# Four constants and the table of settings of a kernel's build-time scheduler: attention and token-mixing MLP on one core

## The chip, the cores and the metric

The kernel runs on one core of a Trainium2 chip. The metric is the device time of one execution in microseconds (us); less is better. TensorE (PE) multiplies matrices, ScalarE (ACT) evaluates activation functions, VectorE (DVE) and GpSimd (POOL) do elementwise work, and SyncE (SP) issues the DMA transfers. Each engine executes its own list of instructions strictly in the order in which the program gives them; between engines there are only semaphores.

## The reference

With x of 2048 rows and 512 columns, 32 heads of 16 columns and F = 1376:

```python
def _A_ref(x, wqkv, wo):
    qkv = (x @ wqkv).reshape(B, S, 3, H, Dh).transpose(2, 0, 3, 1, 4)
    q, k, v = qkv[0], qkv[1], qkv[2]
    p = softmax(einsum("bhqd,bhkd->bhqk", q, k) * Dh ** -0.5)
    o = einsum("bhqk,bhkd->bhqd", p, v)
    return o.transpose(0, 2, 1, 3).reshape(B, S, D) @ wo

def _B_ref(x, w1, b1, w2, b2):
    u = gelu(einsum("bsd,sf->bdf", layernorm(x), w1) + b1)
    return (einsum("bdf,fs->bds", u, w2) + b2).transpose(0, 2, 1)

xn = layernorm(x)
return x + _A_ref(xn, A_wqkv, A_wo) + _B_ref(xn, B_w1, B_b1, B_w2, B_b2)
```

## The kernel before

The work is cut into score steps, numbered 0 to 1023. One step is one tile of 128 keys against 512 queries for two heads: two matmuls of 32 by 128 weights (line 792), each into one bank of PSUM. Two steps make four matmuls that run side by side in the four row strips of TensorE. Thirty-two steps, which are 16 key tiles of four heads, are a block; there are 32 blocks of 512 queries and four heads each. The last block works in two halves of 256 queries (line 782 for its scores).

A finished step then needs its exponentials, 128 x 1024 values, and it can get them in two ways:

- on ScalarE: one activation over both banks when the two banks are neighbours, or two activations of 512 columns each when they are not (line 818). I call such a step an A step.
- on VectorE: one pass that writes the bits of an approximate exponential as 16-bit integers (line 827), followed by three integer "shifts" of that tile (line 833), which give three more terms of the approximation. The shifts may run on VectorE or on GpSimd. I call such a step a D step.

TensorE then multiplies each resulting tile with V (line 874, and line 863 in the last block): four matmuls of 128 by 32 weights over 256 columns, side by side in the four column strips. An A step needs one such group, a D step needs four. Between the scores and this "PV" work lie other column-strip matmuls: projections of Q, K and V and both products of the MLP and the output projection (line 922, in groups of four over 512 columns, and line 978). Changing between the row strips of the scores and the column strips of all else is a mode switch. Lines 715 and 719 are filler matmuls that keep the clock of TensorE up.

The Python program decides the whole order while it is being built. The class `Sched` keeps a clock per engine, a model of what each operation costs, and a main loop that always takes the candidate with the earliest modelled start. The constants of this model stand at the head of the file. `PE_SWITCH` is the cost of a mode switch, `PE_LAT` the time from the start of a matmul of 512 columns to the moment at which its reader may start, the third entry of a `cost=("C", ...)` tuple the time of a matmul group, and `port_time` says when VectorE or GpSimd may start an operation that uses the port that they share. A wrong constant changes no result: the semaphores enforce every dependency. It changes only which operation comes next in the lists.

The choices of the loop have seven knobs. They decide when a step is given to VectorE, how many tile buffers are kept back, how close to ScalarE's next need the scores are put, whether other matmuls come ahead of PV work, how much work VectorE may have waiting, and how many D steps are open at a time. `POLICIES` has 16 sets of the seven. `PLAN` has 64 hexadecimal digits, one for each 16 score steps, and each digit names the set in force during those steps:

```python
d_steal, p_keep, dead_slack, pe_fit, ext_rank, d_back, d_fly = POLICIES[PLAN[plan_at // PLAN_STEP]]
```

The next scores are placed at a time worked out from ScalarE's modelled clock; other matmuls are taken first if they end before it:

```python
need = sc.free["act"] + EXP_I * ahead - 0.46 - dead_slack
go = max(e_s, min(need, t2))
if pick is not None and pick[0] + pick[4] + PE_SWITCH <= go + pe_fit:
    pe_c = pick[:4]
```

Scores of a block may not start before the PV work of the block before the last has been placed in full. When a block's PV work is complete, an epilogue (lines 1096 to 1132) copies it out, divides by the sums, and leaves it for the output projection. The last block has its own end (lines 1141 to 1189).

Of the kernel before, what the change touches and what calls it, by code (L numbers as in the profile page):

```python
# [56 lines left out]


SEM = 0.05
PE_SWITCH = 0.11  # L60
PE_LAT = 0.40
AS_I, AS_L = 0.8, 0.9
EXP_I, EXP_L = 0.904, 1.03
EXPH_I, EXPH_L = 0.477, 0.60
# [25 lines left out]
PLAN_STEP = 16  # L90
PLAN = tuple(int(c, 16) for c in "61cb9804b04216e61600920a2d300db6900a621963f2325ed3a2bc440e00e3d2")
URGENT = ("kv0", "qt", "kt", "vt")
URG_DUE = 24
UT0, UT_STEP = 196, 31
# [29 lines left out]
class Sched:  # L124
# [51 lines left out]
    def keep_clock(self, ready, cost):  # L176
# [3 lines left out]
        if mode != self.pe_mode:  # L180
            t = max(t, self.pe_end + PE_SWITCH)
        for x in tiles:
# [3 lines left out]
        own = "F" if self.pe_mode in ("F", None) else "C"  # L186
        s = self.pe_end + (PE_SWITCH if own != self.pe_mode else 0.0)
        most = int((t - s - (PE_SWITCH if own != mode else 0.0) - FILL_SLACK) / FILL_T)
        have = self.worked(t - HAM_W, t)
# [41 lines left out]

    def port_time(self, eng, t):

        return max(t, self.port_free["pool" if eng == "dve" else "dve"])

    def _time(self, op, cost, ready, port):
        eng = op.eng
# [6 lines left out]
        elif eng == "pe":  # L244
            mode, tiles, dur = cost
            t = max(self.free["pe"], ready)
            if mode != self.pe_mode:
                t = max(t, self.pe_end + PE_SWITCH)
                self.pe_mode = mode
# [7 lines left out]
            self.busy["pe"] += dur * len(tiles) / 4.0  # L257
            op.t0, op.t1 = t, t + dur + PE_LAT - 0.214
            self.pe_work.append((t, dur, len(tiles) / 4.0))
# [122 lines left out]
def bass_parallel_sum__softmax_full_mha__mixer_token_mlp__prompt_kernel(  # L382
# [18 lines left out]
    with ExitStack() as es:  # L401
# [56 lines left out]
        def bank(i):  # L458
            return ps[:, i * 512:(i + 1) * 512]
# [280 lines left out]
        def blk_of(n):  # L740
            if n < 4 * N_TURN:
                kt, b = n // 4, n % 4 // 2
            elif n < 2 * BN:
                b, kt = divmod(n // 2 - 2 * N_TURN, NKT - N_TURN)
                kt += N_TURN
            else:
                b, kt = divmod(n // 2, NKT)
            qb, G = divmod(b, NG)
            T, e_ = divmod(G, 2)
            return b, kt, qb, G, T, e_  # L750
# [3 lines left out]
        def vblk(n):  # L754
            if 4 * N_TURN > n and n % 4 >= 2:
                return -1
            return blk_of(n)[0] if n < N31 else NBLK - 1 + (n - N31) // 16
# [53 lines left out]
        def buf(i, a=0, z=1024):  # L811
            return pT[:, i, a:z] if i < NPB else x_sb[:, :, :].rearrange("p t d -> p (t d)")[:, 1024 * (i - NPB) + a:1024 * (i - NPB) + z]
# [35 lines left out]
        def pv_specs(item, first, last):  # L848
            n, term, p = item
            b, kt, qb, G, T, e_ = blk_of(n)  # L850
            par = n % 2
            vt, vk = (VM, "VM") if term == len(SHIFTS) else (V17, "V")
            spill = (vk, kt, T + 1) if T < 3 else (vk, kt + 1, 0)
            specs = []
            if n >= N31:
                m = (n - N31) % 16
                pb = vblk(n)
                for z in range(2):
                    k_ = 2 * (m // 2) + z
                    for i in range(2):  # L860
                        c = 2 * par + i
                        off = (k_ * H + 8 * T + 2 * c + e_) * 17
                        specs.append(dict(eng="pe", fn=lambda e, c=c, z=z, i=i, off=off: e.matmul(
                            bank(pv_bank[pb])[32 * c:32 * c + 32, 0:256], lhsT=vt[:, off:off + 32],
                            rhs=buf(p, 512 * i + 256 * z, 512 * i + 256 * z + 256), start=first and z == 0, stop=last and z == 1,
                            tile_position=(0, 32 * c)),
                            reads=[(vk, k_, T), ("pT", p), ("pTh", p), ("Vone",), (vk, k_ + 1, 0)], writes=[("bank", pv_bank[pb])], name="pv",
                            cost=("C", (c,), 0.107)))
                return specs
            vb = vblk(n)  # L870
            for c in range(4):
                h, i = divmod(c, 2)
                off = (kt * H + 8 * T + 4 * par + 2 * i + e_) * 17
                specs.append(dict(eng="pe", fn=lambda e, c=c, h=h, i=i, off=off: e.matmul(  # L874
                    bank(pv_bank[vb])[32 * c:32 * c + 32, 256 * par:256 * par + 256], lhsT=vt[:, off:off + 32],
                    rhs=buf(p, 512 * i + 256 * h, 512 * i + 256 * h + 256), start=first, stop=last,
                    tile_position=(0, 32 * c)),
                    reads=[(vk, kt, T), ("pT", p), ("pTh", p), ("Vone",), spill], writes=[("bank", pv_bank[vb])], name="pv",
                    cost=("C", (c,), 0.107)))
            return specs  # L880

        def pv_emit(b, item):
            pv_q[b].remove(item)
            n, term, p = item
            sk = b if b < NBLK - 1 else (b, n % 2)
            first = sk not in pv_started
            pv_started.add(sk)
            pv_left[b] -= 1
            last = pv_left[b] == 0
            if b >= NBLK - 1:  # L890
                par_done[sk] = par_done.get(sk, 0) + 1
                last = par_done[sk] == 8 + 3 * sum(1 for z in on_d if vblk(z) == b and z % 2 == n % 2) and all(
                    z in pbuf or z in on_d for z in range(NN) if z >= N31 and vblk(z) == b and z % 2 == n % 2)
            for s_ in pv_specs(item, first, last):
                add(s_)
            pv_seen.add((b, n % 2))
            if not (term == 0 and shifts_of.get(n, 0) > 0):
                free_p.append(p)
            else:
                w_hold[n] = p  # L900
# [29 lines left out]
        def score_has(n):  # L930
            b, kt, qb, G, T, e_ = blk_of(n)
            return ("q", b - b % 2) in have and (("k", T, kt // 4) in have if T else ("k0", kt) in have)
# [392 lines left out]
        def grp(b):  # L1325
            return max(0, b)
# [39 lines left out]
        def est(specs):  # L1366
            s0 = specs[0]
            r = 0.0
            for s_ in specs:
                r = max(r, sc.ready(s_["eng"], s_["reads"], s_["writes"]))  # L1370
            t = max(sc.free[s0["eng"]], r)
            if s0.get("port"):
                t = sc.port_time(s0["eng"], t)
            return t
# [102 lines left out]
        while True:  # L1477
            if next_n >= plan_at and plan_at < NN:
                d_steal, p_keep, dead_slack, pe_fit, ext_rank, d_back, d_fly = POLICIES[PLAN[plan_at // PLAN_STEP]]
                plan_at += PLAN_STEP  # L1480
# [21 lines left out]
            if ready_q and fly < d_fly and len(free_p) >= 4 + p_keep:  # L1502
                act_free = sc.free["act"]
                for qi, n in enumerate(ready_q):
# [3 lines left out]
                    t = est(sp_)  # L1508
# [41 lines left out]
            t_pe = max(sc.free["pe"], sc.pe_end)  # L1550
            t_c = max(sc.free["pe"], min(sc.pe_tiles.values()) if sc.pe_tiles else 0.0) if sc.pe_mode == "C" else t_pe + PE_SWITCH
            if next_n < NN and pv_grp >= grp(vblk(next_n)) - 1 and len(free_banks) >= 2 + spare and score_has(next_n):
# [4 lines left out]
                if sc.pe_mode != "S":  # L1557
                    e_s = max(e_s, sc.pe_end + PE_SWITCH)
            jobs = []
# [230 lines left out]
```

## Time and profile before

| | |
|---|---|
| median of 3 runs | 701.61 us (701.22 to 702.15) |
| the profiled execution | 701.73 us |
| its span on the core, first to last instruction | 699.9 us |
| TensorE, line 792 (scores) | 272.5 us busy, 1976 matmuls |
| TensorE, line 874 on pT and V (largest group of PV) | 243.9 us busy, 4588 matmuls |
| VectorE, line 827 (D steps) | 261.1 + 106.5 us busy, 342 instructions |
| VectorE, line 833 (shifts) | 124.2 + 56.9 + 51.2 + 13.0 us busy, 583 instructions |
| GpSimd, line 833 (shifts) | 168.0 + 78.2 + 67.8 + 16.7 us busy, 317 instructions |
| granted clock of TensorE | 1.000 |

Busy times are the union of an engine's spans, so for a pipelined engine they are less than count times mean duration: ScalarE's and TensorE's instructions overlap their neighbours, and how fast an engine really goes is read from the distance of successive ends. "Idle before" is the time in which an engine had nothing running just ahead of an instruction, with what ended it.

### The profile page before, as it was taken

What the parts mean: (1) busy time and instruction counts of PE and PEld (TensorE: products, weight loads), DVE (VectorE), ACT (ScalarE), POOL (GpSimd) and SP (SyncE); (2) the same over time, 40 slices, a digit from 0 to 9 for tenths busy, and PEclk for the clock granted to TensorE, in tenths of its full rate; (3) what the DMA queues carried; (4) which work ended last, traced back from release to release, by engine and by line L of the source; (5) the groups of instructions that cost most, each with busy time, mean ns of one, the idle gap of its engine ahead of it and who ended that gap; (6) DMA issues with size and microseconds to landing.
All of it is one profiled execution on the core that took longest, in us unless ns stands there. A gap on an engine that the chain in (4) does not pass through costs nothing.

```text
span 699.9 us, 30143 instructions
## 1 busy us (share of the span) xinstructions
PE 687.6 (98%) x13277; PEld 319.4 (46%) x13277; DVE 658.0 (94%) x1154; ACT 681.0 (97%) x778; POOL 402.9 (58%) x450
## 2 busy tenths in 40 slices
PE   8999999999999999999999999999999999999998
PEld 6554444454444444444444443444443444444444
DVE  6898979989989999999999999899999999999997
ACT  6999999999999999999999999999999999999995
POOL 5856646765535556565555555565565655656553
PEclk9999999999999999999999999999999999999999
DMA  7500131001322212220222112221112122103101
GB/s 219 81 16 18 48 81 24 21 13 25 79 43 52 45 25 48 49 48 22 42 57 65 40 46 64 62 57 38 35 48 46 30 55 61 47 24 75 26 17 43
DMA packets 88997, 33.88 MB, mean 48 GB/s; under 512 B 70754, under 2 KB 88866, under 8 KB 88866
## 3 DMA queue, kind: packets, MB, share of 16 engines
q1 hardware_dynamic: 88050, 31.56, 19.5%
q8 instruction: 104, 1.70, 1.0%
q10 hardware_dynamic: 816, 0.39, 0.2%
q14 instruction: 27, 0.22, 0.1%
HBM read 21.70 MB, written 2.35 MB: 34 GB/s over the span
## 4 chain that ended last, share of the span: by engine, by line
PE 57%; ACT 29%; DVE 10%; POOL 1%; issue 1%; DMA 1%; POOLq 0%
PE ps L792 21%; PE ps L874 20%; ACT pT L818 20%; PE ps L922 13%; ACT x_sb L818 9%; DVE pT L827 3%; DVE pT L833 2%; DVE x_sb L827 2%; PE ps L978 1%; DMA xnT<-hx 1%; DVE x_sb L833 1%; ACT wkv_raw L1034 1%; PE ps L696 0%; PE ps L1262 0%; PE ps L782 0%
## 5 line engine op out<-in xcount | busy, mean ns | idle before, releaser
L818 ACT ACTIVATE pT<-ps 128x1024 bf16<-128x1024 f32 (+1 forms) x550 | 523.1, 1134 | 4.9 <-PE ps L792 4.8
L792 PE MATMUL ps<-QT,KT 32*128 32x512 bf16 x1976 | 272.5, 385 | 4.3 <-DVE pT L827 1.1
L827 DVE TENSOR_SCALAR pT<-ps 128x1024 int16<-128x1024 f32 (+1 forms) x244 | 261.1, 1081 | 11.9 <-PE ps L792 11.3
L874 PE MATMUL ps<-pT,V 128*32 128x256 bf16 x4588 | 243.9, 275 | 1.6 <-DVE V L988 0.4
L833 POOL TENSOR_SCALAR pT<-pT 128x1024 int16<-128x1024 int16 x161 | 168.0, 1043 | 122.7 <-DVE pT L833 75.5
L818 ACT ACTIVATE x_sb<-ps 128x1024 bf16<-128x1024 f32 (+1 forms) x206 | 223.8, 1173 | 0.9 <-PE ps L792 0.8
L792 PEld LDWEIGHTS ps<-QT,KT 32*128 32x128 bf16 x1976 | 76.2, 91 | 177.6 <-ACT pT L818 72.2
L874 PEld LDWEIGHTS ps<-pT,V 128*32 128x32 bf16 x4588 | 110.8, 96 | 74.2 <-issue 54.7
L833 DVE TENSOR_SCALAR pT<-pT 128x1024 int16<-128x1024 int16 x297 | 124.2, 442 | 0.8
L827 DVE TENSOR_SCALAR x_sb<-ps 128x1024 int16<-128x1024 f32 (+1 forms) x98 | 106.5, 1097 | 5.2 <-PE ps L792 4.7
L874 PE MATMUL ps<-x_sb,V 128*32 128x256 bf16 x1708 | 110.8, 275 | 0.4
L833 POOL TENSOR_SCALAR pT<-x_sb 128x1024 int16<-128x1024 int16 x75 | 78.2, 1043 | 50.1 <-DVE pT L833 30.6
L833 POOL TENSOR_SCALAR x_sb<-pT 128x1024 int16<-128x1024 int16 x65 | 67.8, 1043 | 45.6 <-DVE pT L833 31.5
L874 PE MATMUL ps<-pT,VM 128*32 128x256 bf16 x888 | 63.0, 275 | 0.0
L922 PE MATMUL ps<-hx,wblk 128*32 128x512 bf16 x688 | 58.2, 384 | 0.0
L833 DVE TENSOR_SCALAR pT<-x_sb 128x1024 int16<-128x1024 int16 x139 | 56.9, 433 | 0.2
L874 PEld LDWEIGHTS ps<-x_sb,V 128*32 128x32 bf16 x1708 | 44.2, 96 | 24.1 <-issue 17.8
L833 DVE TENSOR_SCALAR x_sb<-pT 128x1024 int16<-128x1024 int16 x116 | 51.2, 449 | 0.5
L922 PE MATMUL ps<-wkv_raw,wblk 128*32 128x512 bf16 x512 | 42.5, 384 | 0.0
L1132 POOL TENSOR_TENSOR oT<-oC,denb 128x256 bf16<-128x256 f32 (+1 forms) x32 | 23.3, 727 | 27.0 <-DVE pT L833 21.7
L874 PEld LDWEIGHTS ps<-pT,VM 128*32 128x32 bf16 x888 | 23.6, 96 | 12.1 <-issue 9.3
L922 PEld LDWEIGHTS ps<-hx,wblk 128*32 128x32 bf16 x688 | 15.6, 95 | 21.2 <-issue 17.4
(124 smaller groups left out, 466.1 us busy)
## 6 DMA issues: line engine op xcount, KB each, us to landing
wblk<-in_B_w_dram SPq DMA_DIRECT2D x10, 512.0 KB, 5.1
wblk<-in_B_w_dram SPq DMA_DIRECT2D x16, 320.0 KB, 3.7
oC<-OT SPq DMA_DIRECT2D x248, 16.0 KB, 1.8
denb<-rden_scratch SPq DMA_DIRECT2D x124, 32.0 KB, 2.4
xr<-in_A_x_dram SPq DMA_DIRECT2D x16, 128.0 KB, 2.3
out_dram<-osb SPq DMA_DIRECT2D x16, 128.0 KB, 1.9
QT<-Qall SPq DMA_DIRECT2D x120, 16.0 KB, 1.8
x_sb<-in_A_x_dram SPq DMA_DIRECT2D x2, 512.0 KB
```

What stands on the lines that cost most here:

```text
L792: specs.append(dict(eng="pe", fn=lambda e, r=r, bk=bk: e.matmul(bank(bk), lhsT=KT[32 * r:32 * r + 32, T, 128 * kt:128 * (kt + 1)], rhs=QT[ ...
L818: return [dict(eng="act", fn=lambda e, cs=cs, src=src: e.activation(buf(pbuf[n])[:, cs], src, ACTF.Exp, scale=LN2_128), reads=[("bank", k) ...
L827: return [dict(eng="dve", fn=lambda e, cs=cs, src=src: e.tensor_scalar(buf_i(w)[:, cs], src, IBIAS, 0.0, ALU.add, ALU.max), reads=[("bank" ...
L833: return dict(eng=eng, fn=lambda e: e.tensor_scalar(buf_i(o), buf_i(w), float(SHIFTS[k]), 1.0, ALU.add, ALU.mult), reads=[("pT", w), ("pTh ...
L874: specs.append(dict(eng="pe", fn=lambda e, c=c, h=h, i=i, off=off: e.matmul(bank(pv_bank[vb])[32 * c:32 * c + 32, 256 * par:256 * par + 25 ...
L922: specs.append(dict(eng="pe", fn=lambda e, c=c, w=w: e.matmul(bank(ex)[32 * c:32 * c + w, :], lhsT=lhs_of(32 * c, 32 * c + w), rhs=rhs, st ...
L978: specs.append(dict(eng="pe", fn=lambda e, ct=ct, c=c, i=i, t=t: e.matmul(bank(ex)[32 * c:32 * c + 32, 128 * i:128 * (i + 1)], lhsT=xnT[:, ...
L1034: yield "act", [dict(eng="act", fn=lambda e, ap=ap: e.activation(ap, ap, ACTF.Gelu_apprx_tanh), reads=[("gT", ft) for ft in fts], writes=[ ...
L1132: yield "pool", [dict(eng="pool", fn=lambda e, cs=cs: e.tensor_tensor(oT[0:m, qb % NOT, T, cs], oC32[0:m, tb_, cs], denb[0:m, tb_, cs], AL ...
```

## The change

The change gives three constants of the model new values, adds one constant, and replaces all the digits of `PLAN`. Nothing else is touched: the sets in `POLICIES`, the operations and the dependencies are the same. Since the lists are worked out from the model, the order of all engines' instructions changes from the first score steps on, and so does the share of the steps that goes to VectorE.

```diff
-PE_SWITCH = 0.11
-PE_LAT = 0.40
+PE_SWITCH = 0.10
+PE_LAT = 0.38
+PV_T = 0.1095
+POOL_AFTER = 0.03
...
-PLAN = tuple(int(c, 16) for c in "61cb9804b04216e61600920a2d300db6900a621963f2325ed3a2bc440e00e3d2")
+PLAN = tuple(int(c, 16) for c in "0005cfbded1bc0b612a3be2c69463c106436663136cad93cd0c524c434c2215b")
...
     def port_time(self, eng, t):
 
-        return max(t, self.port_free["pool" if eng == "dve" else "dve"])
+        return max(t, self.port_free["pool"] if eng == "dve" else self.port_free["dve"] + POOL_AFTER)
...
-                            cost=("C", (c,), 0.107)))
+                            cost=("C", (c,), PV_T)))
...
-                    cost=("C", (c,), 0.107)))
+                    cost=("C", (c,), PV_T)))
```

## The prediction

> **What bounds the kernel now.** I read the shares first, then the groups of ScalarE, then its list in time. The page's shares and groups:
>
> ```profile
> PE 687.6 (98%) x13277; PEld 319.4 (46%) x13277; DVE 658.0 (94%) x1154; ACT 681.0 (97%) x778; POOL 402.9 (58%) x450
> ...
> L818 ACT ACTIVATE pT<-ps 128x1024 bf16<-128x1024 f32 (+1 forms) x550 | 523.1, 1134 | 4.9 <-PE ps L792 4.8
> ...
> L818 ACT ACTIVATE x_sb<-ps 128x1024 bf16<-128x1024 f32 (+1 forms) x206 | 223.8, 1173 | 0.9 <-PE ps L792 0.8
> ```
>
> Three engines look full, and the chain of waits puts 57% on PE. But PE's busy time is a union of modelled, pipelined spans, and the scheduler fits PE's other work in until ScalarE's next need. ScalarE's exponentials have only 5.8 us of idle ahead of them. ScalarE's list in time around one loss (start, length, xcount):
>
> ```profile
> 223.96 7.58 ACT L818 ACTIVATE pT<-ps 128x1024 bf16<-128x1024 f32 x8
> 231.22 1.24 ACT L818 ACTIVATE x_sb<-ps 128x1024 bf16<-128x1024 f32 x1
> 232.12 4.00 ACT L818 ACTIVATE pT<-ps 128x1024 bf16<-128x1024 f32 x4
> 235.73 1.31 ACT L818 ACTIVATE x_sb<-ps 128x1024 bf16<-128x1024 f32 x1
> 236.64 1.32 ACT L818 ACTIVATE pT<-ps 128x1024 bf16<-128x1024 f32 x1
> 237.54 1.33 ACT L818 ACTIVATE x_sb<-ps 128x1024 bf16<-128x1024 f32 x1
> 239.25 6.52 ACT L818 ACTIVATE pT<-ps 128x1024 bf16<-128x1024 f32 x7 [0.38 <-PE ps L792]
> ```
>
> Ends follow each other by 0.917 us (232.46 to 236.12 for four). Over the trace the 1024-column activation has that distance at its median and 75th percentile, 0.918 at the 90th; the 512-column one 0.490. So ScalarE is the bound, and the span can be written as: first exponential of line 818 starts at 14.3; 684 x 0.917 + 72 x 0.490 = 662.5; the four Gelus and the table load before them 6.5 (357.35 to 363.82); lost time 9.1, of which 0.9 is the table load after the Gelus and the first activation behind it; last exponential ends at 692.6, and 7.4 follow. That makes 699.8 of 699.9.
>
> The 8.15 us really lost: where? TensorE and VectorE at the loss above:
>
> ```profile
> 237.04 0.44 PE L792 MATMUL ps<-QT,KT 32*128 32x512 bf16 x4
> ...
> 237.41 1.48 PE L922 MATMUL ps<-hx,wblk 128*32 128x512 bf16 x24
> 237.47 1.23 DVE L827 TENSOR_SCALAR pT<-ps 128x1024 int16<-128x1024 f32 x1
> 237.54 1.33 ACT L818 ACTIVATE x_sb<-ps 128x1024 bf16<-128x1024 f32 x1
> ...
> 238.82 0.49 PE L792 MATMUL ps<-QT,KT 32*128 32x512 bf16 x4
> ```
>
> Two steps are scored, one becomes a D step, so ScalarE has one exponential, 0.917 us, for the 1.78 us until TensorE scores again. I therefore counted, in the order of each engine's instructions, the runs of other matmuls between two scorings, and priced a run by the trace's start distances: 0.1095 for four PV matmuls, 0.2155 for four of line 922, 0.055 for four over 128 columns, and 0.2 for its two mode switches with what hangs on them (last score to first PV matmul 0.315, PV to score 0.205), plus 0.2 for the scores. Outside the Gelus the order has 42 runs over 1.5 us. Fourteen of them follow a pair with a D step, and at those fourteen places, and no others, ScalarE loses over 0.2 us: eight runs of 1.59 lose 0.38 to 0.59 (mean 0.482), four of 1.70 lose 0.499 on the mean, two of 1.81 lose 0.615; 7.08 in all. The 28 that follow two A steps lose at most 0.1. Twelve shorter runs (1.16 to 1.28) behind a D step lose 0.80 together, 0.067 each, the largest 0.165.
>
> **The change, part by part.** The built program gives exact counts; no time of the scheduler's model is used.
>
> (1) ScalarE's load. Activations of 1024 columns go from 684 to 694, of 512 columns from 72 to 56: +10 x 0.917 - 16 x 0.490 = +1.3 us, straight on the bound. Steps given to VectorE fall from 300 to 298.
>
> (2) Long runs behind a D step: from 14 to 5 (three of 1.59, one of 1.70, one of 1.81). By the rows above they lose 3 x 0.482 + 0.499 + 0.615 = 2.6 instead of 7.1: -4.5. Long runs behind two A steps fall from 28 to 21 and cost nothing, the two queued exponentials (1.83 us) cover them; were that cover gone, each would cost about 0.5.
>
> (3) Middle runs (1.16 to 1.49) behind one A step: from 12 to 27. Some follow a single scored step, which the trace of before has only up to 1.07 us. 23 lie within 1.16 to 1.28; I take 0.067 for each, 1.5. Four, of 1.38 to 1.49, have no row: bounds are 0 and the 0.482 of the 1.59 runs, and I take 0.27, halfway between the neighbours, 1.1. Together 2.6 against 0.8: +1.8. Bounds of the difference: 0 if they lose as much in all as the twelve did, +4.9 if each of the 23 loses 0.165 and each of the four 0.482.
>
> (4) The other engines. TensorE: 24 PV matmuls (-0.66) and 18 fillers (-0.3) fewer, but 1,375 instead of 1,358 runs of one mode, 17 switches x 0.1 = +1.7: +0.7 us, hidden behind ScalarE; uncovered it is all on the end. VectorE: 258 to 251 wide and 84 to 94 half passes of line 827 (distances 1.13 and 0.60) and three shifts of 0.335 fewer: -2.9 us. GpSimd: three shifts of 1.04 fewer, with 42% of its span idle. The SP list keeps its 685 entries and no transfer changes size; no wait of line 792 on a transfer shows in the trace. Cost: 0, no gain either, since ScalarE does not wait for them.
>
> (5) The end. Behind the last exponential the chain of before reads (start, length):
>
> ```profile
> 692.19 0.73 POOL oT L1132
> 692.91 0.04 issue
> 692.96 0.77 POOLq L401
> 693.72 0.04 issue
> 693.77 3.23 PE ps L922 x56
> 697.00 0.02 issue
> 697.03 0.69 DVE osb L1141
> ```
>
> GpSimd's last product comes late because VectorE still has the shifts of step 1019, and four output tiles (0.69 each) are all added behind it. In the new order the last D step is 1016, that product is placed before step 1022 is scored, and one output tile is added before the last PV group and one right behind it. Two additions off the chain are worth up to 1.3; bounds 0 and -1.3, I take -0.7.
>
> (6) The start. The first D step is 18 instead of 24, while VectorE still does layer norms: one pass and three shifts, 1.1 + 1.0 us, earlier. ScalarE's first 21 exponentials run without idle now, and VectorE waits 0.72 us at 27.3 within them, so I take 0; bounds 0 and +1.0.
>
> Sum: +1.3 - 4.5 + 1.8 - 0.7 = -2.1 us. Against the profiled execution: 701.7 - 2.1 = 699.6; its time stands 0.1 above the median of the runs, so the median becomes 699.5 us.
>
> The Trainium skill, TensorEngine Tiling (Array Packing), Key Properties, speaks against the change: changing the tiling mode drains TensorE. The trace agrees, with 0.315 us from the last score matmul to the first PV matmul against 0.2155 between groups without a change. By that rule alone the 17 extra switches come out on the end, as in the second rival (703.6 us); by the rows of ScalarE they are hidden and the sum stays 699.6.
>
> **The rivals.** (A) The losses move instead of going: 15 middle runs more, and ScalarE short behind each. For it: in the new order such runs come in rows (steps 558 to 606 and 654 to 676), so that no backlog builds up between them. Against: in the rows of before (steps 207 to 219, 272 to 291) single losses were 0.03 to 0.17. At the upper bound of (3) the sum is +1.3 - 4.5 + 4.9 - 0.7 = +1.0 with the end's gain, 702.6, which is no change.
>
> (B) TensorE becomes the bound. Place: all of the steady stretch, where TensorE waits little; its start distances exceed the floors above by 15 to 20 us in the whole span. Price: +0.7 of its own work, and it meets a floor once ScalarE's losses fall. It decides if that slack cannot be used because it sits at waits for banks: then the long runs' loss returns as later scores, (2) is worth nothing, and the load of (1) with TensorE's 0.7 stays: 701.6 + 2.0 = 703.6, slower.
>
> (C) The change does what the counts say and the middle runs cost nothing more: -2.1 - 1.8 = -3.9, 697.7, or 697.1 with the end's best. For it: six of the 23 follow single steps, so that the scores behind them are only one step late.
>
> **How the numbers follow.** What a measurement of this kernel tells from no change is about 0.2%, 1.4 us: faster is below 700.2, slower above 703.0. The forecast has 0.5, C 0.17, A 0.17, B 0.16. Of the forecast's 0.5 about 0.05 falls above 700.2. Faster: 0.45 + 0.17 = 0.62; same: 0.05 + 0.17 = 0.22; slower: 0.16. The forecast's own range is 698.3 to 700.7, half the bounds of (3) and (5). The range for 8 in 10 goes from 697.0 (C with the end's best) to 703.3, which takes in A with the worst start and the near part of B.
>
> **What would show it.** Right: activations 694 + 56 with ends 0.917 apart; idle ahead of line 818 falling from 5.8 us to 2 to 4; losses over 0.35 at about five places, behind pairs with a D step; the last exponential ending near 691 and under 7.0 us behind it; VectorE's chain no longer in the last 20 us. Wrong: losses over 0.35 behind two A steps, or ahead of step 64; the distance 0.917 itself changed; idle of ScalarE as large as before, or put down to buffers (line 874) instead of scores.

## The result and the profile after

The changed kernel takes 700.03 us (median of 12 runs, 699.5 to 701.33) against 701.19 us (12 runs, 700.83 to 702.15) for the kernel before: ratio 0.9982, 95% interval 0.9974 to 0.999. That is 1.2 us less by the medians and 0.18% by the ratio: faster beyond the interval, and a little under the 0.2% that the prediction took as the least difference that can be told. The forecast was 699.5 us.

The page of the changed kernel, its shares and the two groups of exponentials (all lines past the head of the file are two further down, so 818 is now 820 and 792 is 794):

```profile
PE 686.3 (98%) x13235; PEld 318.2 (46%) x13235; DVE 653.6 (94%) x1154; ACT 682.3 (98%) x772; POOL 400.7 (57%) x447
...
L820 ACT ACTIVATE pT<-ps 128x1024 bf16<-128x1024 f32 (+1 forms) x539 | 517.5, 1140 | 3.2 <-PE ps L794 3.0
...
L820 ACT ACTIVATE x_sb<-ps 128x1024 bf16<-128x1024 f32 (+1 forms) x211 | 225.2, 1144 | 0.7 <-PE ps L794 0.4
```

The shares tell nothing: all engines look as full as before. What moved is the idle time ahead of the exponentials, from 5.8 to 3.9 us, as was forecast (2 to 4). The more exact ledger is ScalarE's: its load (activations of 1024 columns x 0.917 plus those of 512 columns x 0.490), the time lost where an end follows the end before it later than that, the start of the first exponential of line 820, and what is left behind the last one. The Gelus and their table loads are the same 7.9 us in both. With them a row adds up to its span within 0.4. All in us, from one profile each:

| | load | lost | of it at places over 0.35 | first exponential | behind the last | span |
|---|---|---|---|---|---|---|
| before | 662.5 | 8.2 | 7.1 (14) | 14.3 | 7.4 | 699.9 |
| after | 663.8 | 6.3 | 4.3 (8) | 13.4 | 6.4 | 697.7 |
| after, a second profile | 663.8 | 7.0 | 4.9 (9) | 14.2 | 6.4 | 699.2 |

One loss in the changed kernel, all engines in time (start, length, xcount, and in brackets the idle time with what ended it):

```profile
193.98 1.23 DVE L829 TENSOR_SCALAR pT<-ps 128x1024 int16<-128x1024 f32 x1
194.04 1.16 ACT L820 ACTIVATE pT<-ps 128x1024 bf16<-128x1024 f32 x1
...
194.54 0.21 PEld L924 LDWEIGHTS ps<-xnT,wq_sb 128*32 128x32 bf16 x8
194.65 0.60 PE L924 MATMUL ps<-xnT,wq_sb 128*32 128x512 bf16 x8
...
195.24 0.11 PEld L794 LDWEIGHTS ps<-QT,KT 32*128 32x128 bf16 x4 [0.48 <-ACT pT L820]
195.25 0.41 PE L794 MATMUL ps<-QT,KT 32*128 32x512 bf16 x4
...
195.68 1.02 ACT L820 ACTIVATE pT<-ps 128x1024 bf16<-128x1024 f32 x1 [0.48 <-PE ps L794]
```

Of a pair, one step went to VectorE and one to ScalarE. The next scores (weights loaded at 195.24) waited for that very exponential, which ended at 195.20 and gave its two banks back; the next exponential then waited for those scores. It is a ring: exponential, bank, scores, exponential. TensorE fills the wait with other matmuls, which is the long run that the prediction counted. Run and bank end almost together. Of the eight places over 0.35, seven follow a pair with a D step. At five of the seven the bank that came last was held by VectorE's pass, at two by the exponential; and the scores start 0.31 to 0.44 us behind the start of the last group of the run, where 0.31 is the least distance between such a group and scores in this trace. So the scores waited at most 0.13 us longer for the bank than for the run, and at two places (235.26 and 451.84) not at all. In the kernel before VectorE's pass held the bank at 11 of the 14 places. Whether a free second pair of banks would by itself have saved the loss is not shown: no run here parts the two.

The end of the changed kernel, the chain of waits behind the last exponential (start, length), which ended at 691.3:

```profile
691.47 0.15 PE ps L865 x2
...
691.76 0.46 DVE denb L1181
...
692.37 0.65 DVE osb L1143
693.02 0.34 DVE OT L1186
...
693.39 0.32 DVE denb L1191
...
693.75 0.43 PE ps L924 x4
...
694.21 0.69 DVE osb L1143
694.90 0.60 DVEq L403
```

GpSimd's late product is gone from it, and so is the row of 56 output matmuls behind it. Two additions of an output tile stand in it; in the kernel before, three of the four additions ran beside those 56 matmuls and only the last stood in the chain. The end is 0.9 us shorter.

### The profile page after: what moved, and what is told of

It reads as the page before. It is cut to its first block, busy times and chain, and to the rows that moved or that the text cites. A ratio compares the mean times of both kernels' runs of the same rounds, so it can differ in the third digit from the quotient of the medians.

```text
span 697.7 us, 30042 instructions
## 1 busy us (share of the span) xinstructions
PE 686.3 (98%) x13235; PEld 318.2 (46%) x13235; DVE 653.6 (94%) x1154; ACT 682.3 (98%) x772; POOL 400.7 (57%) x447
## 4 chain that ended last, share of the span: by engine, by line
PE 61%; ACT 22%; DVE 15%; issue 1%; POOL 1%; DMA 0%; SPq 0%; DVEq 0%; POOLq 0%
PE ps L876 23%; PE ps L794 21%; ACT pT L820 15%; PE ps L924 14%; ACT x_sb L820 7%; DVE pT L829 6%; DVE pT L835 3%; DVE x_sb L829 2%; DVE x_sb L835 1%; PE ps L865 1%; PE ps L980 1%; PE ps L784 1%; POOL pT L835 0%; PE ps L717 0%; DVE OT L1098 0%
## 5 line engine op out<-in xcount | busy, mean ns | idle before, releaser
L820 ACT ACTIVATE pT<-ps 128x1024 bf16<-128x1024 f32 (+1 forms) x539 | 517.5, 1140 | 3.2 <-PE ps L794 3.0
L829 DVE TENSOR_SCALAR pT<-ps 128x1024 int16<-128x1024 f32 (+1 forms) x251 | 266.7, 1074 | 14.2 <-PE ps L794 13.5
L794 PE MATMUL ps<-QT,KT 32*128 32x512 bf16 x1976 | 276.9, 384 | 2.6 <-DVE pT L829 0.5
L835 POOL TENSOR_SCALAR pT<-pT 128x1024 int16<-128x1024 int16 x173 | 180.5, 1043 | 124.8 <-DVE pT L835 83.6
L829 DVE TENSOR_SCALAR x_sb<-ps 128x1024 int16<-128x1024 f32 (+1 forms) x94 | 99.6, 1071 | 6.3 <-PE ps L794 6.1
L835 POOL TENSOR_SCALAR pT<-x_sb 128x1024 int16<-128x1024 int16 x61 | 63.6, 1043 | 48.1 <-DVE pT L835 36.6
L835 POOL TENSOR_SCALAR x_sb<-pT 128x1024 int16<-128x1024 int16 x58 | 60.5, 1043 | 43.1 <-DVE pT L835 33.0
L835 DVE TENSOR_SCALAR pT<-x_sb 128x1024 int16<-128x1024 int16 x127 | 51.9, 434 | 0.4
L835 DVE TENSOR_SCALAR x_sb<-pT 128x1024 int16<-128x1024 int16 x112 | 47.2, 429 | 0.3
L835 POOL TENSOR_SCALAR x_sb<-x_sb 128x1024 int16<-128x1024 int16 x22 | 23.0, 1043 | 16.9 <-DVE pT L835 15.2
```

What stands on the lines that cost most here:

```text
L794: specs.append(dict(eng="pe", fn=lambda e, r=r, bk=bk: e.matmul(bank(bk), lhsT=KT[32 * r:32 * r + 32, T, 128 * kt:128 * (kt + 1)], rhs=QT[ ...
L820: return [dict(eng="act", fn=lambda e, cs=cs, src=src: e.activation(buf(pbuf[n])[:, cs], src, ACTF.Exp, scale=LN2_128), reads=[("bank", k) ...
L829: return [dict(eng="dve", fn=lambda e, cs=cs, src=src: e.tensor_scalar(buf_i(w)[:, cs], src, IBIAS, 0.0, ALU.add, ALU.max), reads=[("bank" ...
L835: return dict(eng=eng, fn=lambda e: e.tensor_scalar(buf_i(o), buf_i(w), float(SHIFTS[k]), 1.0, ALU.add, ALU.mult), reads=[("pT", w), ("pTh ...
```

## Experiments

**The table and the constants apart.** Two kernels, each with one half of the change:

```diff
 new_constants_old_table: the changed kernel with
-PLAN = ... "0005cfbded1bc0b612a3be2c69463c106436663136cad93cd0c524c434c2215b"
+PLAN = ... "61cb9804b04216e61600920a2d300db6900a621963f2325ed3a2bc440e00e3d2"

 old_constants_new_table: the kernel before with
-PLAN = ... "61cb9804b04216e61600920a2d300db6900a621963f2325ed3a2bc440e00e3d2"
+PLAN = ... "0005cfbded1bc0b612a3be2c69463c106436663136cad93cd0c524c434c2215b"
```

> The four constants of the change with the table of before. By the counts (ScalarE is the bound; its load and the runs that leave it short decide): 661 activations of 1024 columns and 128 of 512 are 668.9 us against 663.8 for the change, 7 long runs behind a pair with a D step instead of 5: about +5.6, near 705.6 us, slower than both kernels. If the constants by themselves carry the gain: 699.5 to 701. If TensorE sets the end, the number of single-mode runs hardly moves, so about 700 to 701.

> The constants of before with the table of the change. By the counts: 628 activations of 1024 columns and 208 of 512 are 677.8 us, +14.0 against the change, four long runs behind a D step instead of five: about +13.4, near 713.4 us. If the table by itself carries the gain: 699.5 to 701. If TensorE sets the end: 700 to 702.

Measured: 705.95 us (ratio to the kernel before 1.0068, 1.0053 to 1.0083) and 716.53 us (1.0217, 1.0201 to 1.0232). Both are slower than either kernel, in the order and near the size that the counts gave: 0.3 and 3.1 us more. The ledgers: load 668.9, lost 6.2, span 703.8; and load 677.8, lost 8.4, span 714.7. The second one's load was exact and its losses were underestimated by some 2.5 us. Neither half carries the gain. Most of the harm is activations of 512 columns: 128 and 208 of them against 56, that is, steps whose two banks were not neighbours.

**One constant put back.** The same with the smallest step that the change makes:

```diff
 old_latency: the changed kernel with
-PE_LAT = 0.38
+PE_LAT = 0.40
```

> The changed kernel with one of the four constants put back: PE_LAT = 0.40. By the counts ScalarE's load grows little (640 activations of 1024 columns and 162 of 512, 666.3 us, +2.4), but long runs behind a pair with a D step go from 5 to 14 and middle ones from 27 to 34, which by the rows is +7 us of lost time: about +9.5, near 709.5 us, with some 8 more places at which ScalarE loses over 0.35. If only the load counts: 702.4. If 0.02 us in a model's constant is too little to matter: 700.

Measured: 710.41 us, 1.0125 (1.011 to 1.014). Load 666.3 and losses of 14.1 us, 19 places over 0.35 instead of 8. This one separates the two terms: of the 11.7 us between the two profiled spans the load explains 2.5 and the losses 7.8, and the rest is a later first exponential and a longer end. (The medians differ by 10.4 us, and by 10.0 if each is taken against the kernel before beside it.) What ScalarE waited for:

```profile
ACT pT L820 <- PE ps L794: 7.9, 15, 0.9
...
ACT x_sb L820 <- PE ps L794: 1.6, 4, 0.5
```

(time in all, times, longest: 9.5 us against 3.0 and 0.4 in the changed kernel). Two hundredths of a microsecond in a model, on the same chip with the same operations, are worth 10 us here. That each early choice of the scheduler changes all that follow, so that the table no longer fits, is the likely reason; it is argued and not shown.

**Which engine sets the time.** Three kernels keep every list of the changed kernel as it is and add idle work to one engine each:

```diff
 more_scalar
+            if side(n) and n % 28 == 3:
+                e.activation(spare_row[:, :], src[:, 0:512], ACTF.Exp, scale=LN2_128)
 more_tensor (ahead of every 17th PV group that is neither first nor last of its sum)
+            for c in range(4):
+                e.matmul(<the group's bank and rows>, lhsT=zer[:], rhs=<the group's tile>, start=False, stop=False)
 more_vector (ahead of every 4th second shift on VectorE)
+                e.tensor_scalar(spare_row_i[:, :], buf_i(w)[:, 0:512], 1.0, 1.0, ALU.add, ALU.mult)
```

> The changed kernel with 27 more activations of 512 columns on ScalarE, spread evenly, into a row that nobody reads; every other list as it is. 27 x 0.490 = 13.2 us of work. If ScalarE is the bound: +10.5 to +13.5 us, 710.5 to 713.5, its few losses shrinking a little. If TensorE is the bound: under +4 us, since TensorE does nothing more.

> The changed kernel with 103 more groups of four PV-shaped matmuls with weights of zero, spread evenly, added into banks that are being summed; every other list as it is. 103 x 0.1095 = 11.3 us of work on TensorE alone. If ScalarE is the bound, what TensorE waits at scores (some 8 us over the start distances' floors) takes part of it: +2 to +6 us, 702 to 706. If TensorE is the bound: +10 to +11.5 us, 710 to 711.5.

> The changed kernel with 73 more integer passes of 512 columns on VectorE, spread evenly, into a row that nobody reads; every other list as it is. Each is between half and all of a shift (0.17 to 0.335 us), so 12 to 24 us of VectorE's time, of which VectorE is idle 44 in the span. If ScalarE is the bound and VectorE has room: +1 to +8 us, 701 to 708, through banks that D steps give back later. If VectorE is a bound as full as ScalarE: at least +12 us.

| | work added | median | against 700.03 | ratio to before |
|---|---|---|---|---|
| more_scalar | 27 x 0.490 = 13.2 | 712.16 | +12.1 (92%) | 1.0157 (1.0142 to 1.0173) |
| more_tensor | 103 x 0.1095 = 11.3 | 702.97 | +2.9 (26%) | 1.0022 (1.0012 to 1.0032) |
| more_vector | 73 x 0.200 = 14.6 | 709.21 | +9.2 (63%) | 1.0109 (1.0092 to 1.0125) |

The 0.200 is the median distance of the added passes' ends to the ends before them (the least is 0.146); VectorE's busy time rose by 13.8 us. The kernel before took 701.89 us beside more_vector, where it took 701.19 beside the 700.03, so by the ratios more_vector's rise is 8.9 us. So ScalarE is the bound, almost one to one; most of the missing part is losses that shrank from 6.3 to 5.6. TensorE, at 98% busy on the page, is not: three quarters of what it was given vanished, and the second rival falls. VectorE is the surprise. It lets ScalarE wait nowhere by name, yet 63% of its extra work came out: ScalarE's losses rose from 6.3 to 15.1 us, with 80 pieces over 0.03 us instead of 26, since a D step's pair of banks, and with it the next scores, comes back as late as VectorE is: the weight loads of the scores waited 51.1 us for VectorE's passes instead of 39.5. The added rows as one view of more_vector has them (count; least, median and most ns; first and last start):

```profile
L839 DVE TENSOR_SCALAR spare_row<-pT x53: 224/284/735, 30.4 to 692.5; 128x512 int16<-128x512 int16 x53
L839 DVE TENSOR_SCALAR spare_row<-x_sb x20: 222/282/748, 62.4 to 675.6; 128x512 int16<-128x512 int16 x20
```

**Tables chosen by the counts.** If the ledger is right, it should be able to rank schedules before they run. Three kernels tried that; more_d_steps has one more condition in the scheduler as well:

```diff
 table_by_counts
+PLAN = ... "0005cfbded1bc0b612a3be2c69463c106436663136cad93cd0c523c4f4c22352"
 more_d_steps
+PLAN = ... "26e14f037967da6e7233036823ec7dfbce39ec6303626f6f7bd26707658e285d"
-                if rel > next_n or nurg or len(free_banks) < 1 + spare or (not urg and others):
+                if rel > next_n or nurg or len(free_banks) < 1 + spare or (not urg and others) or (nm == 'qt' and others and due - next_n > 4):
 table_with_end
+PLAN = ... "0005cfbded1bc0b612a3be2c69463c104436663136cad93cdfc524c034c62ba6"
```

> The changed kernel with another table, chosen for the least sum of ScalarE's load and the priced runs. Against the change: 689 activations of 1024 columns and 62 of 512 (662.2 us, -1.6), four long runs instead of five and 28 middle ones instead of 27 (-0.4), last D step 1019 instead of 1016 as in the kernel before (+0.9): 698.9 us if ScalarE's counts are all. VectorE gets 4.3 us more (six more shifts, two more D steps); if its work costs 60% on the end, as the run with more integer passes showed, +2.6: near 701.5. If counts no longer order such close schedules: anywhere from 699 to 703.

> The changed kernel with a table and one more condition (a Q projection does not start while another task of matmuls holds a bank, until it is nearly due) that give VectorE 13 more D steps, 311 instead of 298. ScalarE's load falls to 653.5 us (656 activations of 1024 columns, 106 of 512; -10.3); long runs 12 instead of 5 and middle ones 36 instead of 27 (+6.7 by the rows). By ScalarE's counts alone 697 to 698 us, faster than both kernels. VectorE gets 32 us more, all but 12 of its 44 us of idle time: if it is nearly as full a bound, at 60% of that, +19: 712 to 718.

> The changed kernel with a third table, chosen for ScalarE's load, the priced runs, VectorE's load and the work placed behind the last exponential together. Against the change: load 663.8 us as before it (695 of 1024, 54 of 512), long runs four instead of five and middle ones 23 instead of 27 (-0.6), three PV groups behind the last exponential as in the change, VectorE within 0.1 us: 0.6 us under the change, 699.4. If the counts miss another place: 700 to 703.

more_d_steps took 721.89 us (1.0288, 1.0274 to 1.0302), over every case of its forecast: ScalarE's load fell to 653.5 us as counted, but its losses rose to 31.4 us, and 13.2 us were left behind the last exponential. This way of giving ScalarE's steps to VectorE did not shorten the kernel. VectorE's busy time rose by 26.8 us to 680.4, but it still stood idle 39.5 us, and the scores' weight loads waited less for its long passes than in the changed kernel (29.6 us instead of 39.5), so that a full VectorE is the cause is not shown; the table and the condition changed at the same time. The largest loss stands at the start, where the first D step is now 6 and VectorE still does layer norms:

```profile
14.01 2.89 ACT L820 ACTIVATE pT<-ps 128x1024 bf16<-128x1024 f32 x3
21.02 3.90 ACT L820 ACTIVATE pT<-ps 128x1024 bf16<-128x1024 f32 x6 [4.12 <-PE ps L794]
```

table_by_counts took 704.51 us (1.0041, 1.0027 to 1.0055), where the counts of ScalarE alone gave 698.9 and those with VectorE 701.5. The place missed is the end: 12.2 us behind the last exponential instead of 6.4, since the scheduler had left much PV work there: 84 PV matmuls start behind the last exponential, against 4 in the changed kernel, with an MLP product ending just before them. Its chain of waits (start, length):

```profile
691.86 1.51 PE ps L924 x28
693.37 1.53 PE ps L865 x56
694.90 3.02 PE ps L924 x56
697.92 1.15 PE ps L865 x21
...
701.02 0.43 PE ps L924 x4
...
701.48 0.69 DVE osb L1143
```

The 2.6 us that the forecast put on VectorE's extra work do not show: VectorE was busy 657.4 us instead of 653.6, and without the three places that the last section describes (2.6 us) ScalarE lost about as much as in the changed kernel.

With that term counted too, table_with_end came to 702.03 us (1.0003, 0.9994 to 1.0012), 2.6 over what was expected and 1.3 over the changed kernel beside it: its end took 7.4 us although as few PV groups stood in it, and it lost 7.4. The last D step is 1019 again, as in the kernel before, and GpSimd's late product is back in the chain:

```profile
691.13 0.72 POOL oT L1134
...
692.70 1.03 PE ps L924 x13
```

This fits the product as what lengthens the end: 7.4 us with it in both kernels, 6.4 without. Between schedules that differ by 1 us the counts do not decide; none of these versions beats the change.

**The changed kernel once more.**

> The changed kernel once more beside it, unchanged. Its load of 663.8, its losses (within 0.3 us of 6.0) and its end (6.4) should come back, place by place; only the start of the first exponential should move, between 13.4 and 14.4. Median within 0.5 of 700.0.

Measured: 700.71 us against 701.82 for the kernel before beside it, 0.9982 (0.9973 to 0.9991), so the ratio came back. The median is outside what was expected (within 0.5 of 700.0), and so is the sum of the losses, 7.0 instead of 6.0. The losses came back place by place and within 0.03 us nearly everywhere (196.7: 0.590 and 198.4: 0.592; 453.3: 0.626 and 455.0: 0.625), but for three: one at 24 us was 0.07 us in the first profile and 0.82 in the second, one at 103 us 0.21 and 0.31, one at 647 us 0.60 and 0.46. The start of the first exponential was 13.4 and 14.2 us. The two profiles of one program differ by 1.5 us in span, nearly all of it in the first 25 us.

## Why the prediction was right or wrong

**The bound** was read rightly, as the three kernels with added work show.

**(1) ScalarE's load**, +1.3: exact, 694 + 56 activations with the same distances of 0.917 and 0.490.

**(2) Long runs**, -4.5: the five were there and lost 0.59, 0.63, 0.63, 0.45 and 0.60, 2.9 us against the 2.6 priced. At the exponential that follows a long run behind two A steps ScalarE lost nothing.

**(3) Middle runs**, +1.8: the 27 lost 2.4 us where 2.6 was taken, but by two errors that cancel. The four between 1.38 and 1.49 lost 0.45, 0.44, 0.23 and 0.47, 1.6 us instead of 1.1, so they are nearer to the long runs than halfway. The other 23 lost 0.8 instead of 1.5, 0.035 each. Their price came from a misread row: the twelve of the kernel before did not lose 0.80. At the exponentials that the scores behind them let start, they lost 0.17 in all, the largest 0.083. The 0.165 that the prediction names belongs to an exponential that began before those scores did and waited for a PV matmul to give back its output tile:

```profile
284.76 1.02 ACT L818 ACTIVATE x_sb<-ps 128x1024 bf16<-128x1024 f32 x1
...
285.07 0.39 PE L792 MATMUL ps<-QT,KT 32*128 32x512 bf16 x2
```

So the middle runs made a difference of +2.2, and all losses but those of the long runs +2.3. The first rival, that such runs in rows cost more, would have cost +4.9: the row from step 558 to 606 lost 0.6 us. One of the 23 lost 0.25, more than the 0.165 that the upper bound allowed to each.

**(4) The other engines**, cost 0: nearly right for TensorE's switches (26% of 0.7 us, an estimate from more_tensor, is 0.2) and wrong as a rule for VectorE. That ScalarE waits for VectorE nowhere by name is not that VectorE has room: it sits one link further back in the ring of banks, and 63% of an addition comes out. Then VectorE's 2.9 us less work may have been a gain of up to 1.8 us that the sum leaves out. No run takes this work away alone. Against it: more_vector's cost came above all in pieces between 0.03 and 0.35 us (8.4 us instead of 1.9), and those grew from the kernel before to the change, from 1.0 to 1.9.

**(5) The end**, -0.7: it was -0.9. The late product of GpSimd fits as the cause, as given: table_with_end, in which it is back, has the old length of the end again. The price was taken from the wrong row: the four additions were not what the chain held, but the 56 matmuls behind the product.

**(6) The start**, taken as 0 with a bound of +1.0: a loss at 24 us which in the kernel before did not show was 0.06 or 0.07 us in four profiles of kernels that share this start and 0.64 to 0.82 in four others. TensorE stood 0.70 us there in the second profile, ahead of a matmul on a tile that a DMA had transposed, and not in the first. The view puts that wait down to VectorE's cast of V (line 1277), but in the first profile the same matmul starts before that cast. That the landing of the transfer moves is the likely reason and was not tested.

By its own profiles the sum is -2.2 us in span from the first pair, as forecast (-2.1), and -0.7 with the second profile of the changed kernel. The medians say -1.2. That the first pair meets the forecast is luck: 0.9 of its 2.2 us is the earlier start of the first exponential, which no term of the sum held. Load +1.3, long runs -4.2, all other losses +2.3 and the end -0.9 make -1.5, so the arithmetic on the steady part held to about 0.6 us; what it lacked was that one profile of each kernel carries about 1 us of chance from the start, and that the loss at 24 us belongs to the new order. With that loss at its mean over the eight profiles, some 0.4 us, -1.5 becomes -1.2, an estimate that agrees with the medians. The third rival, that the middle runs cost nothing more, fell.

Of the signs named ahead, the idle time, the end and the chain of its last 20 us came as written. Two did not: losses over 0.35 stood at eight places instead of about five, and one of them, at 40.3 us behind step 35, is ahead of step 64, which the prediction had named as a sign of being wrong. It is one of the four middle runs, so the sum had a price for it; the sign was drawn too narrowly.

What stays open: whether the four constants are better as such. How either table was found is not on record; the two crossed kernels show only that each table does better with its own constants.

## What to carry to other kernels

When several engines read 95% busy, take the distances of successive ends on each: here one of them sat at a fixed distance nearly always, and the time was its count times that distance plus the places where it slipped; adding idle work to one engine at a time then showed which it was. An engine that nobody waits for by name can still be nearly a bound when it holds a buffer that the next link needs. The settings of this build-time scheduler did well only with the model constants that they came with: change the two together, judge by measured time, and read the work left behind the bound's last instruction as a term of its own. Give a loss to a cause only if the cause ends before the loss begins; the misread row of the middle runs came from not doing so.

## What the runs showed of the hardware that was not expected

One profile of table_by_counts took 707.03 us while its other runs took 704.15 to 704.83. In it TensorE stood 1.51 us for a shift on GpSimd, and about a microsecond after that its granted clock fell to half for 3.4 us (103.7 to 107.1). The wait, and the stretches around it (length, busy time of PE, PEld, DVE, ACT, POOL with counts, clock, DMA share, GB/s):

```profile
102.78 0.29 PE L876 MATMUL ps<-pT,VM 128*32 128x256 bf16 x4 [1.51 <-POOL pT L835]
```

```profile
100.00:103.00 3.00, 1.49 (x30) 0.64 (x26) 3.00 (x5) 2.50 (x4) 2.70 (x4) 1.00 0.20 39
103.00:106.00 3.00, 3.00 (x86) 1.94 (x82) 1.79 (x5) 1.94 (x2) 0.81 (x1) 0.62 0.55 127
106.00:109.00 3.00, 3.00 (x48) 1.06 (x46) 1.54 (x4) 2.28 (x3) 2.38 (x3) 0.82 1.32 231
```

PE busy fell to 1.49 of 3 us, then the clock was 0.62 and 0.82 in the next stretches, and ScalarE lost 2.6 us at three exponentials there: 1.05 from the wait itself, before the fall, and 1.56 behind it. The changed kernel has a wait of 0.70 us at the same place, and its clock stayed at 1.00. In no other profile did TensorE stand longer than 0.94 us behind the first 12 us, and none shows such a fall between its start and its last microseconds. The Trainium skill, TensorE: Matmul & The Clock Gate, Why this matters for your kernels, warns of idle gaps over about 3 us between bursts of matmuls. In this profile one of 1.5 us within a lightly filled stretch went with the fall. It was seen once and not provoked again; that the wait caused the fall is not shown.
